# Granule 4's values one piece sooner and its last norm ahead of the key copies, mask tables later, two PSUM banks changed in granule 2, and three squares moved to VectorE

## The chip, the cores and the metric

One core of a Trainium2 chip. The metric is device time in microseconds (us) of one execution; lower is better. A run lists the time and the span from the first to the last instruction; the time is about 1.8 us more than the span.

## The reference, cut to what matters

```python
scores = q @ k.T / sqrt(64) - slope[h] * dist          # 4 batches, 8 heads, 768 positions
scores = where(is_global | is_local, scores, -1e9)     # 8 global keys, 96 local ones
a = exp(scores - max); a = a / (sum(a) + 1e-9)
x = (a @ v)  as 3072 x 512
h = maximum(x @ w_in, 0)                               # 512 x 2048
out = (s * h * h + b) @ w_out                          # 2048 x 512
```

## The kernel before: the parts concerned

The kernel works through 12 granules of 256 positions. Granule j+1's attention is interleaved by hand with the first product (P1, eight pieces) of granule j and the second product (P2) of granule j-1. The order of the calls is the order of the instructions on every engine. Terms: `SS` makes scores (PE), exponentials (ACT) and masked weights (DVE); `A` multiplies by the values and then normalises (DVE); `KO`/`VO` copy neighbouring keys and values (DVE); `XT_dma`/`XT_pe` transpose the normalised result for P1; `T_ev` copies transposes out of PSUM; `make_tmpl(h)` makes one head's mask table (ACT); `Q` squares a P1 piece later on (DVE); `W_tw` subtracts blocks of output weights for the later granules (DVE, below "table difference"); `P2_bias` adds the bias to an output (DVE). PE is TensorE, ACT ScalarE, DVE VectorE.

```python
ps_h  = tc.tile_pool(name="ps_h",  bufs=2, space=PSUM)   # "psh": two buffers
ps_o  = tc.tile_pool(name="ps_o",  bufs=1, space=PSUM)   # "pso": one
ps_av = tc.tile_pool(name="ps_av", bufs=1, space=PSUM)   # "av": one
...
def P1(j, fp, sq="dve", tag="psh"):
    ...                                  # 8 matmuls into ps
    flush()                              # squares that wait in `pend` (DVE)
    nc.scalar.activation(gs, ps, Relu)   # ACT
    if sq == "act":    nc.scalar.activation(gs, gs, Square)
    elif sq == "late": late_sq[j, fp] = gs     # Q(j, fp) squares it on DVE later
    else:              pend.append(gs)
...
    def period(j, items, at, late=None, mid=()):     # j = 3 and 4
        SS(j, (0, 1));  run(items, at[0])
        A(j, 0);        run(items, at[1])
        A(j, 1, "psh"); run(list(mid), 100)
        SS(j, (2, 3));  run(items, at[2])
        A(j, 2)
        KO(j + 1)
        run(items, at[3])
        A(j, 3, "psh")
        if late is None: XT_dma(j)
        ...                                          # VO, XB, then the rest of items
```

Later granules (`steady`) run a tighter loop, which the change leaves alone; its first P1 piece of granule 4 reads what `XT_dma(4)` made.

The softmax here doesn't subtract the row's maximum and nothing guards it: scores larger than these inputs give would overflow.

## Time and profile before

| | before |
|---|---|
| time, three runs at first | 210.44 us median (210.06 to 210.52) |
| span of the profiled run | 207.9 us |
| PE busy | 200.8 us (97%) |

To read it: a P1 matmul's row is 0.273 us long on average, but the next one starts 0.109 us after it, so rows overlap and "busy" hides short stops. PE's losses below are therefore from start to start, as in the prediction (usual spacing 0.109 us for 256 columns, 0.216 for 512). A gap of one spacing exactly inside a group of four or eight is a missing record, not a stop: this trace has all 2291 matmuls.

### The profile page before, as it was taken

The numbers are of one execution on the slowest core, as the hardware profiler recorded it, in microseconds if no ns is written. First come the engines' busy times: TensorE is split into PE (matmuls) and PEld (weight loads), VectorE is DVE, ScalarE is ACT, GpSimd is POOL, SyncE is SP. The second block draws the span as 40 slices with busy tenths as digits, with TensorE's granted clock in tenths as the row PEclk, the third lists the DMA queues.
The fourth block names the chain that finished last, engine by engine and source line by source line (L and its number), as shares of the span: only waits on it lengthen the run. The fifth ranks groups of instructions, "written<-read, shape, count | busy, mean of one in ns | idle before, by whom it ended". The sixth has DMA issues, their size and how long they took to land.

```text
span 207.9 us, 5598 instructions
## 1 busy us (share of the span) xinstructions
PE 200.8 (97%) x2291; PEld 160.8 (77%) x2291; DVE 167.9 (81%) x404; ACT 119.8 (58%) x184; POOL 75.5 (36%) x98
## 2 busy tenths in 40 slices
PE   7999999999999998999999999999999999999992
PEld 2667866557666777888988988988978988988882
DVE  3776567599889998788799799788799799787683
ACT  5779899345978784636536536546356456425300
POOL 8985673937364006509029019037000000000000
PEclk9999999999999999999999999999999999999999
DMA  5999999999999976999969959959946040040022
GB/s 165 193 184 198 188 196 190 182 145 160 134 131 166 182 133 85 183 144 132 209 93 118 208 83 119 207 101 120 193 79 176 3 151 4 0 151 3 2 104 101
DMA packets 103850, 27.64 MB, mean 133 GB/s; under 512 B 91408, under 2 KB 101904, under 8 KB 103824
## 3 DMA queue, kind: packets, MB, share of 16 engines
q0 software_dynamic: 70976, 13.11, 86.3%
q1 hardware_dynamic: 31792, 13.64, 32.1%
q10 hardware_dynamic: 1056, 0.52, 0.9%
q8 instruction: 18, 0.29, 0.6%
q14 instruction: 8, 0.07, 0.1%
HBM read 27.26 MB, written 6.29 MB: 161 GB/s over the span
## 4 chain that ended last, share of the span: by engine, by line
PE 79%; ACT 9%; DVE 5%; DMA 4%; issue 2%; SPq 0%; ACTq 0%; DVEq 0%
PE ps L528 35%; PE ps_w L690 14%; PE ps_wb L690 6%; PE ps L589 6%; PE ps_av L446 4%; PE ps_s L395 4%; PE ps_wa L690 3%; ACT pt L408 3%; ACT gT L538 2%; DMA xT<-xn 2%; DMA raw<-in_k_dram 2%; PE ps_s L379 2%; PE ps_2s L589 2%; DVE xn L464 1%; ACT gT L546 1%
## 5 line engine op out<-in xcount | busy, mean ns | idle before, releaser
L528 PE MATMUL ps<-xT,w_in_bf 128*128 128x256 bf16 x768 | 96.5, 273 | 1.0 <-DMA xT<-xn 0.6
L528 PEld LDWEIGHTS <-w_in_bf 128*128 128x128 bf16 x768 | 72.9, 98 | 12.4 <-DMA xT<-xn 0.9
L540 ACT ACTIVATE gT<-ps 128x512 bf16<-128x512 f32 x72 | 43.0, 598 | 59.1 <-PE ps L528 56.3
L408 ACT ACTIVATE pt<-ps_s 128x1024 bf16<-128x1024 f32 (+1 forms) x48 | 43.0, 952 | 2.0 <-PE ps_s L395 2.0
L690 PEld LDWEIGHTS <-sw 128*128 128x128 bf16 x288 | 28.1, 98 | 3.4
L418 DVE TENSOR_TENSOR pt<-pt,tmpl 128x1024 bf16<-128x1024 bf16 (+1 forms) x40 | 25.2, 647 | 2.9 <-ACT pt L408 2.4
L556 DVE TENSOR_TENSOR gT<-gT 128x512 bf16<-128x512 bf16 x66 | 25.1, 416 | 1.8 <-ACT gT L540 1.6
L690 PEld LDWEIGHTS <-gT 128*128 128x128 bf16 x216 | 20.5, 98 | 3.3 <-issue 0.2
L112 POOL DMA_DIRECT2D vaug<-in_v_dram x24 | 21.5, 911 | 4.1 <-DMA w_out_bf<-in_moe_w_out_dram 1.7
L125 POOL COPY pdum<-xT 1x1 bf16<-1x1 bf16 x5 | 4.7, 944 | 48.6 <-DMA xT<-xn 48.6
L464 DVE TENSOR_TENSOR xn<-ps_av,rc 128x256 bf16<-128x256 f32 x48 | 20.4, 425 | 1.7
L589 PE MATMUL ps<-w_out_bf,gT 128*128 128x512 bf16 x80 | 19.7, 379 | 0.0
L690 PE MATMUL ps_w<-tw,sw 128*128 128x256 bf16 x144 | 18.7, 272 | 0.0
L700 DVE SCALAR_TENSOR_TENSOR u<-ps_w,s_bc,bvec 128x256 f32<-128x256 f32 x27 | 12.9, 480 | 6.7 <-PE ps_w L690 6.7
L446 PEld LDWEIGHTS <-pt 128*128 128x128 bf16 x352 | 15.3, 98 | 3.3 <-DVE xn L464 1.0
L104 POOL DMA_DIRECT2D qnat<-in_q_dram x18 | 16.1, 905 | 2.8 <-DMA w_out_bf<-in_moe_w_out_dram 1.4
L538 ACT ACTIVATE gT<-ps 128x512 bf16<-128x512 f32 x24 | 14.2, 598 | 4.4 <-PE ps L528 4.4
L446 PE MATMUL ps_av<-vaug,pt 128*128 128x65 bf16 x224 | 16.4, 193 | 0.3 <-DVE xn L464 0.2
L104 POOL DMA_DIRECT2D knat<-in_k_dram x18 | 16.0, 894 | 1.2 <-issue 1.0
L463 DVE RECIPROCAL rc<-ps_av 128x4 f32<-128x4 f32 x48 | 8.7, 182 | 9.2 <-PE ps_av L446 9.0
L589 PEld LDWEIGHTS <-gT 128*128 128x128 bf16 x96 | 8.6, 98 | 8.2
L395 PE MATMUL ps_s<-qT,kT 64*128 64x128 bf16 x224 | 12.4, 218 | 0.0
(94 smaller groups left out, 241.1 us busy)
## 6 DMA issues: line engine op xcount, KB each, us to landing
out_dram<-o_pr SPq DMA_DIRECT2D x8, 512.0 KB, 4.1
vaug<-in_v_dram POOLq DMA_DIRECT2D x24, 128.0 KB, 7.8
knat<-in_k_dram POOLq DMA_DIRECT2D x22, 128.0 KB, 5.7
qnat<-in_q_dram POOLq DMA_DIRECT2D x22, 128.0 KB, 7.7
w_in_bf<-in_moe_w_in_dram POOLq DMA_DIRECT2D x8, 256.0 KB, 8.2
w_out_bf<-in_moe_w_out_dram POOLq DMA_DIRECT2D x4, 512.0 KB, 9.9
out_dram<-o_pr SPq DMA_DIRECT2D x7, 256.0 KB, 5.3
raw<-in_q_dram ACTq DMA_DIRECT2D x2, 256.0 KB, 4.9
```

What stands on the lines that cost most here:

```text
L104: nc.gpsimd.dma_start(t[:, i, :, :], src[b, :, sb * P : (sb + 1) * P, :].rearrange("h p d -> p h d"))
L112: nc.gpsimd.dma_start(vaug[b % 2][:, sb, :, 0:D], v[b, :, sb * P : (sb + 1) * P, :].rearrange("h p d -> p h d"),)
L395: nc.tensor.matmul(ps[:, hi, oc * P : (oc + 1) * P], lhsT=kt[r, :], rhs=qT[j][r, hp, i * P : (i + 1) * P], start=not biased, stop=not bias ...
L408: nc.scalar.activation(pt[:, :, 0:n], ps[:, :, 0:n], ACT.Exp, scale=QSCALE)
L418: nc.vector.tensor_tensor(pt[:, :, 0:n], pt[:, :, 0:n], m, ALU.mult)
L446: nc.tensor.matmul(av[:, i, hi, :], lhsT=pt[:, hi, c * P : (c + 1) * P], rhs=vv, start=n_ == 0, stop=n_ == len(ops) - 1,)
L464: nc.vector.tensor_tensor(xn[j][:, :, 2 * hp : 2 * hp + 2, :], av[:, :, :, 0:D], rc[:].to_broadcast((P, GB, 2, D)), ALU.mult,)
L528: nc.tensor.matmul(ps[:, i, :], lhsT=w_in_bf[:, kc, fc * P : (fc + 1) * P], rhs=xT[j][:, kc, :], start=(kc == 0), stop=(kc == KC - 1),)
L540: nc.scalar.activation(gs.rearrange("p f (r t) -> p f r t", r=2), ps[:].rearrange("p f (t r) -> p f r t", r=2), ACT.Relu,)
L556: nc.vector.tensor_tensor(gs, gs, gs, ALU.mult)
L589: nc.tensor.matmul(po[j, tb], lhsT=gT[j][:, fc, tb * P : (tb + 1) * P], rhs=w_out_bf[:, fc, :], start=(fc == 0), stop=(fc == FC - 1),)
L690: nc.tensor.matmul(wt[j, ps], lhsT=lhs[:, f, :], rhs=rhs[:, f, :], start=first and f == 0, stop=f == HF - 1, skip_group_check=True,)
```

## The change

Its intent: ACT makes mask tables when PE does not wait for it; granule 2's last values need not wait for a norm in the same bank; granule 4's normalised result is ready sooner, so that its DMA transposes land before P1 asks for them. One square of granule 3's period and two of granule 4's go from ACT to DVE.

```diff
+    P1(1, 2)
+    P1(1, 3)
     make_tmpl(2)
-    P1(1, 2)
-    make_tmpl(3)
-    P1(1, 3)
     P1(0, 6)
-    make_tmpl(4)
     T_quads(2, "k", ("pso", "av"))
...
     T_ev(2, 1, "q", "act")
+    make_tmpl(3)
     P1(1, 4)
     KO(2)
     VO(2)
-    make_tmpl(5)
+    make_tmpl(4)
     P1(1, 5)
     SS(2, (0, 1))
     P1(1, 6)
     P1(1, 7)
+    make_tmpl(5)
     make_tmpl(6)
...
-    A(2, 3)
+    A(2, 3, "psh")
...
-    XT_pe(2, "act", "psh")
+    XT_pe(2, "act", "av")
...
         A(j, 2)
-        KO(j + 1)
+        if at[3]:
+            KO(j + 1)
         run(items, at[3])
         A(j, 3, "psh")
+        if not at[3]:
+            KO(j + 1)
...
-            (P1, 2, 4, "act"),
+            (P1, 2, 4),
...
-   items += [(P2, l, 5), (P2_bias, 1, 0), (P1, m, 2, "act"), (P2, l, 6), (P1, m, 3, "act"), (P1, m, 4, "act")]
-   items += [(P2, l, 7), (P1, m, 5, "act"), ...]
-   period(j, items, (4, 3, 3, 0), mid=...)
+   items += [(P2, l, 5), (P2_bias, 1, 0)]
+   items += [(P1, m, 2, "late"), (P1, m, 3, "late"), (P2, l, 6), (Q, m, 2), (Q, m, 3)]
+   items += [(P1, m, 4, "act"), (P2, l, 7), (P1, m, 5, "act"), ...]
+   period(j, items, (4, 2, 3, 0), mid=...)
```

More of the change, by code (lines that the diff above doesn't have):

```diff
@@ L1074 @@
             items = [(P1, m, 0, "act"), (P2, l, 4), (P1, m, 1), (W_tw, 2, 0, 4)]
-            items += [(P2, l, 5), (P2_bias, 1, 0), (P1, m, 2, "act"), (P2, l, 6), (P1, m, 3, "act"), (P1, m, 4, "act")]
-            items += [(P2, l, 7), (P1, m, 5, "act"), (P1, m, 6), (W_tw, 4, 0, 4), (P1, m, 7), (W_sw, m, 3), (flush,), (W_tw, 4, 4, 8)]
-            period(j, items, (4, 3, 3, 0), mid=((W_tw, 2, 4, 8), (P2_bias, 1, 1, False)))
+            items += [(P2, l, 5), (P2_bias, 1, 0)]
+            items += [(P1, m, 2, "late"), (P1, m, 3, "late"), (P2, l, 6), (Q, m, 2), (Q, m, 3)]
+            items += [(P1, m, 4, "act"), (P2, l, 7), (P1, m, 5, "act"), (P1, m, 6), (W_tw, 4, 0, 4), (P1, m, 7), (W_sw, m, 3), (flush,), (W_tw, 4, 4, 8)]
+            period(j, items, (4, 2, 3, 0), mid=((W_tw, 2, 4, 8), (P2_bias, 1, 1, False)))
         else:
```

## The prediction

> **What bounds the kernel now.** I read the page's first part, then the chain that ended last, then the table of windows, then the timeline of the tensor engine (PE) beside those of VectorE (DVE) and ScalarE (ACT). The busy shares first:
>
> ```profile
> PE 200.8 (97%) x2291; PEld 160.8 (77%) x2291; DVE 167.9 (81%) x404; ACT 119.8 (58%) x184; POOL 75.5 (36%) x98
> ```
>
> PE is busy for 97%, and the chain of waits is PE for 79%. No matmul is added or removed by the change, so it can win only time in which PE stands still. The windows (us: length, then busy time of PE, PEld, DVE, ACT, POOL) show where that could be:
>
> ```profile
> 20.00:30.00 10.00, 9.66 (x152) 8.13 (x151) 5.82 (x15) 9.12 (x17) 7.36 (x10) 1.00 1.57 193
> ...
> 60.00:70.00 10.00, 10.00 (x110) 6.43 (x109) 9.69 (x21) 6.81 (x11) 4.66 (x6) 1.00 2.32 143
> 70.00:80.00 10.00, 9.18 (x98) 7.02 (x96) 9.36 (x21) 8.18 (x12) 0.19 (x1) 1.00 0.95 160
> 80.00:100.00 20.00, 19.94 (x241) 17.61 (x239) 16.42 (x42) 11.15 (x18) 11.68 (x14) 1.00 1.38 143
> ```
>
> From 20 to 30 us ACT is the full engine (9.12 of 10); from 60 to 80 us it is DVE (9.69 and 9.36); after 80 us PE hardly stops. So the change, which touches only granules 2, 3 and 4, has 20 to 80 us to work on. Four lines of PE's timeline there carry its waits (in brackets: idle time, releaser):
>
> ```profile
> 29.00 0.44 PE L288 MATMUL ps_t<-ident,qnat 64*64 64x64 bf16 x30 [0.28 <-ACT kT L308]
> ...
> 40.48 0.20 PE L446 MATMUL ps_av<-vaug,pt 128*128 128x65 bf16 x1 [0.18 <-DVE xn L464]
> ...
> 56.72 1.91 PE L528 MATMUL ps<-xT,w_in_bf 128*128 128x256 bf16 x16 [0.15 <-ACT gT L538]
> ...
> 79.74 1.92 PE L528 MATMUL ps<-xT,w_in_bf 128*128 128x256 bf16 x16 [0.61 <-DMA xT<-xn]
> ```
>
> The brackets understate the loss, as a matmul is still shown busy while its result drains. I therefore took it from start to start: in the chain of waits eight L528 matmuls take 0.87 us, so 0.109 apart; four L589 take 0.86. The distance to the next start, less the matmul's own spacing, gives the loss: 0.49 at 28.50-29.00 (q transposes of granule 2), 0.21 at 26.18 (a P1 piece), 0.35 at 40.48 (last values of granule 2), 0.36 at 56.72, 0.31 at 72.59 (last values of granule 4), 0.77 at 79.74 (first P1 of granule 4, which needs the transposed xn). About 2.5 us in all; that is the ceiling of what the change aims at.
>
> Granule 4 stands under a second bound, which decides the size:
>
> ```profile
> 69.30 0.42 DVE L464 TENSOR_TENSOR xn<-ps_av,rc 128x256 bf16<-128x256 f32 x1
> ...
> 69.64 0.68 DVE L651 TENSOR_TENSOR tw<-w_out_bf,tw 128x1024 bf16<-128x1024 bf16 x1
> ...
> 70.24 0.69 DVE L627 TENSOR_TENSOR o_pr<-o_pr,bvec 128x512 f32<-128x512 f32 x1
> ...
> 70.93 0.69 DVE L418 TENSOR_TENSOR pt<-pt,tmpl 128x1024 bf16<-128x1024 bf16 x1
> ...
> 71.85 0.69 DVE L418 TENSOR_TENSOR pt<-pt,tmpl 128x1024 bf16<-128x1024 bf16 x1 [0.22 <-ACT pt L408]
> ```
>
> The reader is to see that each begins where the last ends: DVE itself, not its inputs, sets when the masked weights for the last values are ready; only 0.22 of it is a wait for ACT.
>
> **What the Trainium skill says.** "Perfetto Trace Analysis", Identifying the Most-Contended Engine, says matmul busy share is no good measure, and under Optimization Strategy that regimes with different full engines are to be found and the gaps read one by one; the windows agree, with three regimes. "PSUM — Partial Sum Buffer", PSUM bank collisions raise a hardware error, says two engines may not touch one bank and quadrant at once, even at different columns. That fits the 29.00 line: the q transposes write another half of the tile that ACT still copies k from, and they wait for that copy. "Perfetto Trace Analysis", Matmuls, wants independent groups in different banks so that eviction overlaps the next group; the 40.48 line is that case missed, two value pieces in the single "av" buffer. "ScalarE: Activation LUTs", Rules for kernel authors, prefers DVE for multiplication: the trace agrees (square 0.63 us on ACT, about 0.42 on DVE), but it helps only where DVE has room.
>
> **The change, part by part.**
>
> *Mask tables later (20 to 38 us).* Eight tables stay eight. An exp for a table occupies ACT for 0.62 us start to start, an eviction 0.49 to 0.60. Now three tables stand before granule 2's k copy on ACT, afterwards one. By hand: the evictions of P1(1,2) and P1(1,3) go at 25.29 and 26.17 instead of 25.54 and 26.64; the P1 piece at 26.18 starts at 25.97; one table from 26.66 to 27.28, one eviction to 27.77, then the k copy until 28.35 (28.95 before). The q transposes can finish from about 28.4 instead of 29.00, so the next P1 piece goes at 28.75 instead of 29.37: 0.62 won. But the two tables moved ahead of granule 2's exponentials, and DVE's work, take a part back: its first score exponential goes at about 31.6 instead of 32.05, 0.46 won. Three squares on DVE (34.63 to 35.72 before) and one norm then let the second values start at 35.9 instead of 36.37. The tables that now wait behind, 5 to 7, end at about 36.4 and the next scores arrive at 36.75, so this third table on ACT is free. Left of this part: about 0.45 us.
>
> *Granule 2's last values in another bank.* At 40.48 they waited for the norm of the pair before in the same bank. "psh" has two buffers, one held by an output sum, the other free. 0.35 us is won. The transposes in "av" find that bank free, as its reader is through; they cost nothing. Sum up to 48 us: **0.8 us**.
>
> *Granule 3, one square to DVE.* ACT loses 0.63 us at 55.56, but the next eviction waits on its own matmuls until about 55.98 and went at 56.09: **0.1 us** won. DVE takes the 0.42 us in a hole of 0.41 before the norm at 56.17.
>
> *Granule 4.* Before the last values there is one P1 piece fewer (0.87 us), and the norms pass the key copies (0.42 and 0.18). Two squares leave ACT (2 x 0.63) and come to DVE (2 x about 0.4). I follow DVE, on the clock of the kernel before: the norm at 69.09 already came straight after DVE's bias from 68.49, so earlier values don't speed it. It runs on through table sum and bias to the masked weights, which come at 71.65 and 72.25 instead of 71.62 and 72.54; the first is unchanged; at the second the 0.22 wait for ACT goes, with the instruction start-up that it exposed: 0.3 won. PE, now at the values by 71.2, waits about 0.5 there and 0.4 at the last ones, more than the 0.31 before. Then the last norm, no longer behind the key copies, ends at 73.35 instead of 74.22, so the xn transposes start about 0.9 us sooner and, if they take as long, land near 78.8 instead of 79.69. PE has 0.87 us more work to do until it needs them, arrives at 72.25 + 6.15 + 0.87 = 79.3 (6.15: from 72.59 to 78.97, where the wait for the transposes began, less 0.23 at 78.1 for a square), and does not wait: 79.74 - 79.3, about **0.45 us** won of the 0.77. Its squares after the values put DVE a little later, but the piece they feed starts at 78.4 and needs the last square at 78.1.
>
> Sum: 0.8 + 0.1 + 0.45 = 1.35 us. I take 0.15 off for the first rival: **1.2 us**, 210.44 - 1.2 = **209.2 us**.
>
> **The rivals.** *A transfer becomes the wait.* Granule 3's q transposes land by the trace's landing events at 48.87 and 50.67 us, PE needs them at 51.68; 0.8 us sooner is 50.9, so 0.2 us of slack remain, and loads of granule 5, paced by an output piece, start sooner and share the DMA engines. Each transpose takes about 2 us there. One late half microsecond would leave only about 0.9 us of gain in all: 209.5. *DVE becomes the bound outright in granule 4.* It gets 3 squares more between 55 and 76 us. If they delay granule 5's masking, which stands behind them, the gain there goes to nothing: 209.6 to 210. For it: 9.69 busy of 10; against it: 80 to 100 us has DVE at 16.42 of 20, and the values of granule 5 need the masking only at 81. *PE absorbs all.* The steady stage is PE-bound, so what comes before should carry to the end unchanged; but if its loads or the two-buffer "psh" re-form the same bubble, the result is 210.4. *The full ceiling:* all of 26-80 us vanishing would give about 208.
>
> **Range and chances.** Runs before lie within 210.06 to 210.52, so 0.25 us is noise. Full working plus a bit of luck gives 208.6, the two rivals together 210.2. Range 208.5 to 210.3. Faster by over 2% would need 4.2 us, more than the 2.5 that stand still; slower by as much would need a wait that no order here shows. So within 2%: 0.98.
>
> **What would show it.** In the changed profile: the k copy on ACT done near 28.4 and the wait of the q transposes nearly gone; the last values of granule 2 unreleased by a norm; xn's transposes issued near 72.5 us (74.29 less 0.9 for the earlier norm and 0.9 won before this stage) and no DMA wait of PE at the first P1 of granule 4; in its place waits of the values for DVE's masked weights. After 80 us the same steps, shifted. The prediction is wrong if PE waits for granule 3's transposes near 51 us, if DVE's chain from 62 to 72 us shrinks more than I think, or if the steady stage opens gaps.

## The result, and the profile after

The changed kernel took **208.20 us** (median of 4 runs, 208.09 to 208.29), beside 210.25 us for the kernel before (4 runs, 209.66 to 210.52). The ratio is 0.9906 (95% interval 0.9882 to 0.993). Ratios here are the mean time of one kernel's fast runs over that of the other's in the same rounds, so not quite the ratio of the medians. It is the same by the 2% mark, faster by 0.9%, and below the forecast range (208.5 to 210.3).

The busy shares after, and the same windows as before (length, then busy PE, PEld, DVE, ACT, POOL):

```profile
PE 199.6 (97%) x2283; PEld 160.6 (78%) x2291; DVE 168.7 (82%) x407; ACT 118.4 (57%) x181; POOL 73.9 (36%) x98
```

```profile
20.00:30.00 10.00, 10.00 (x155) 8.51 (x151) 6.30 (x16) 8.43 (x17) 7.31 (x10) 1.00 1.56 193
...
60.00:70.00 10.00, 9.71 (x105) 6.52 (x106) 9.73 (x21) 7.16 (x11) 3.70 (x5) 1.00 2.04 147
70.00:80.00 10.00, 9.75 (x102) 7.49 (x102) 9.40 (x22) 6.33 (x10) 3.52 (x5) 1.00 1.19 172
80.00:100.00 20.00, 19.94 (x240) 17.60 (x238) 16.56 (x43) 11.21 (x18) 7.67 (x10) 1.00 1.47 144
```

What to see: PE's loss left the stretches 20 to 30 us and shrank from 70 to 80 us (9.18 busy before, 9.75 after), a smaller one came up at 60 to 70 us, where PE had been full, and DVE is still full there. PE's timeline after, at the places of the four lines quoted in the prediction and at two new ones:

```profile
28.20 0.55 PE L288 MATMUL ps_t<-ident,qnat 64*64 64x64 bf16 x32
...
39.59 0.19 PE L446 MATMUL ps_av<-vaug,pt 128*128 128x65 bf16 x1
...
55.75 0.49 PE L528 MATMUL ps<-xT,w_in_bf 128*128 128x256 bf16 x3
...
68.81 1.05 PE L528 MATMUL ps<-xT,w_in_bf 128*128 128x256 bf16 x8 [0.18 <-DVE xn L464]
...
71.21 0.20 PE L446 MATMUL ps_av<-vaug,pt 128*128 128x65 bf16 x1 [0.18 <-DVE pt L418]
...
78.46 0.71 PE L528 MATMUL ps<-xT,w_in_bf 128*128 128x256 bf16 x5
```

The q transposes are one unbroken group now (0.11 us lost from start to start, 0.49 before); the last values of granule 2 follow the matmuls ahead of them at once; the first P1 of granule 4 (last line) names no DMA. In return a P1 piece waits at 68.81 for a norm on DVE, which holds its PSUM buffer (0.34 us start to start), and the last values of granule 4 wait for masked weights at 71.21 (0.34 us, 0.31 before).

ACT in the kernel before, then after, up to granule 2's k copy (L308):

```profile
26.02 0.74 ACT L255 ACTIVATE tmpl<-base 128x640 bf16<-128x640 bf16 x1
26.64 1.21 ACT L538 ACTIVATE gT<-ps 128x512 bf16<-128x512 f32 x2
27.75 0.73 ACT L255 ACTIVATE tmpl<-base 128x640 bf16<-128x640 bf16 x1
28.37 0.58 ACT L308 COPY kT<-ps_t 128x512 bf16<-128x512 bf16 x1
```

```profile
26.58 0.73 ACT L255 ACTIVATE tmpl<-base 128x640 bf16<-128x640 bf16 x1
27.20 0.59 ACT L538 ACTIVATE gT<-ps 128x512 bf16<-128x512 f32 x1
27.68 0.59 ACT L308 COPY kT<-ps_t 128x512 bf16<-128x512 bf16 x1
```

The copy ends 0.68 us sooner by the clock (28.95 against 28.27); 0.09 of it was there at the unchanged P1 piece at 21.6 us. DVE in the kernel before at granule 4's key copy and last norm, and the issue of its xn transposes (SPq is SyncE, which issues DMAs):

```profile
73.05 0.42 DVE L339 COPY ko<-kT 128x1024 bf16<-128x1024 bf16 x1
...
73.80 0.42 DVE L464 TENSOR_TENSOR xn<-ps_av,rc 128x256 bf16<-128x256 f32 x1
...
74.29 2.51 SPq L507 DMA_TRANSPOSE xT<-xn  x2
```

And after, with the last masks:

```profile
69.87 1.28 DVE L418 TENSOR_TENSOR pt<-pt,tmpl 128x1024 bf16<-128x1024 bf16 x2
...
71.89 0.42 DVE L464 TENSOR_TENSOR xn<-ps_av,rc 128x256 bf16<-128x256 f32 x1
72.23 0.42 DVE L339 COPY ko<-kT 128x1024 bf16<-128x1024 bf16 x1
...
72.38 2.50 SPq L507 DMA_TRANSPOSE xT<-xn  x2
```

The key copy now follows the last norm, and the transposes are issued 1.9 us sooner by the clock. By the trace's landing events the second one landed at 76.11 us, 79.69 before. From marks of PE (starts of matmuls that both kernels have in the same order), the length of each stage:

| stage, between starts on PE | before | after | won |
|---|---|---|---|
| P1(0,5), at 21.6 us, to P1(0,6) | 4.58 | 4.38 | 0.20 |
| to granule 2's first scores | 5.04 | 4.66 | 0.38 |
| to its second scores | 5.48 | 5.62 | -0.14 |
| to its xn transposes | 4.89 | 4.53 | 0.36 |
| to granule 3's scores | 10.08 | 10.08 | 0 |
| to granule 4's scores | 11.58 | 11.52 | 0.06 |
| to granule 5's scores | 13.17 | 13.63 | -0.46 |
| to the first P1 of granule 4, 79.7 us before | 3.31 | 2.54 | 0.77 |
| to the same place in the next period, 94 us | 14.42 | 14.41 | 0.01 |

Together 1.2 us (94.16 - 21.60 less 92.87 - 21.51). Of the -0.46, the two waits of 0.34 us less the 0.31 of before make 0.37, and another 0.06 lies at the values between them. The 1.2 us are less than the 2.05 us between the medians. Whence the rest, and whether each part does what the table says, was for the experiments.

### The profile page after: what moved, and what is told of

It is laid out like the page before. It is cut to its first block, busy times and chain, and to the rows that moved or that the text cites. A ratio compares the mean times of both kernels' runs of the same rounds, so it can differ in the third digit from the quotient of the medians.

```text
span 206.5 us, 5590 instructions
## 1 busy us (share of the span) xinstructions
PE 199.6 (97%) x2283; PEld 160.6 (78%) x2291; DVE 168.7 (82%) x407; ACT 118.4 (57%) x181; POOL 73.9 (36%) x98
## 4 chain that ended last, share of the span: by engine, by line
PE 83%; DVE 8%; DMA 3%; ACT 3%; issue 1%; POOL 0%; SPq 0%; DVEq 0%; ACTq 0%; POOLq 0%
PE ps L528 37%; PE ps_w L690 14%; PE ps_wb L690 6%; PE ps L589 6%; PE ps_s L395 5%; PE ps_av L446 5%; PE ps_wa L690 4%; DMA raw<-in_k_dram 2%; PE ps_s L379 2%; DVE xn L464 2%; PE ps_2s L589 2%; DVE pt L418 2%; ACT pt L408 1%; DMA xT<-xn 1%; DVE o_pr L627 1%
## 5 line engine op out<-in xcount | busy, mean ns | idle before, releaser
L556 DVE TENSOR_TENSOR gT<-gT 128x512 bf16<-128x512 bf16 x68 | 25.8, 415 | 1.8 <-ACT gT L540 1.6
L112 POOL DMA_DIRECT2D vaug<-in_v_dram x24 | 21.6, 918 | 4.4 <-DMA w_out_bf<-in_moe_w_out_dram 1.7
L125 POOL COPY pdum<-xT 1x1 bf16<-1x1 bf16 x5 | 3.2, 648 | 49.2 <-DMA xT<-xn 49.2
L589 PE MATMUL ps<-w_out_bf,gT 128*128 128x512 bf16 x74 | 18.8, 379 | 0.4 <-issue 0.2
L395 PE MATMUL ps_s<-qT,kT 64*128 64x128 bf16 x224 | 12.5, 218 | 0.0
```

The lines of the kernel that those rows point to most:

```text
L112: nc.gpsimd.dma_start(vaug[b % 2][:, sb, :, 0:D], v[b, :, sb * P : (sb + 1) * P, :].rearrange("h p d -> p h d"),)
L395: nc.tensor.matmul(ps[:, hi, oc * P : (oc + 1) * P], lhsT=kt[r, :], rhs=qT[j][r, hp, i * P : (i + 1) * P], start=not biased, stop=not bias ...
L556: nc.vector.tensor_tensor(gs, gs, gs, ALU.mult)
L589: nc.tensor.matmul(po[j, tb], lhsT=gT[j][:, fc, tb * P : (tb + 1) * P], rhs=w_out_bf[:, fc, :], start=(fc == 0), stop=(fc == FC - 1),)
```

## The experiments

All ran correct. Sixteen runs of eleven kernels (the kernel before and the changed one among them); the first twelve runs in three sets of five rounds beside the kernel before, the last four as looks. The sets ran on chips 12, 14 and 10, the looks on chip 11. Each run left one trace, so the stages of one kernel rest on one trace; for the kernel before there are six traces, for the changed one three.

### Is the gain as large as first measured?

**The kernel before against itself** (no edit):

> The kernel before, unchanged, against itself. Theory A (the forecast's sum was right in size and the four runs of before were scattered: 209.66 to 210.52): same, ratio within 0.2% of 1, and times around 209.7. Theory B (before is really about 210.3 and its profiled run, 209.63, was a lucky one): same ratio, but times of 210.2 to 210.5, and a trace with a span near 208.5 instead of 207.9, which should then show an extra wait of 0.5 to 0.8 us, most likely for the xn transposes of granule 4 or granule 3's q transposes.

Ratio 1.0009 (0.9988 to 1.003); 210.01 us (209.49 to 210.29), beside 209.89 (209.32 to 210.38) in the same rounds. Its trace repeats the table's stages within 0.01 us up to 80 us; then it loses 0.45 us at one P1 piece at 94 us, waiting for xn transposes. The times lie between the two theories.

**The changed kernel again** (no edit), in two sets:

> The changed kernel again, with more rounds. Theory A: 1.1 to 1.4 us below before in the same rounds (ratio 0.9935 to 0.9948), the sum of the shifts that the two traces show in granules 2 to 4. Theory B: 2.0 us below (ratio 0.9906).

Ratio 0.9932 (0.991 to 0.9954), 208.48 us: 1.4 us below before. As theory A said; its stages again sum to 1.2 us.

> The changed kernel again, to settle the size of the gain: the traces' steps add to 1.2 us, while its ten runs so far lie 1.5 us below before by the span. If the steps are all there is, the ratio here is near 0.994 (1.2 to 1.3 us); if before loses more to late DMA landings in the runs that were not profiled, it stays near 0.9925 (1.5 us or more).

Ratio 0.9922 (0.9892 to 0.9951), 208.56 us. The third set doesn't settle it by itself: before had one run of 211.59 in it, and before's mean was 210.18 us, against 209.83 and 209.78 in the other two sets. Its stages, from 21.6 to 94 us, last 71.33 us, against 72.56 before: 1.23 us.

### The parts of granule 2

**Tables and banks** (both edits of granule 2, nothing else):

> Only the tables moved and granule 2's last values and transposes in other PSUM banks. Theory A: 0.65 us below before (the two traces: 0.90 us of shift at 41 us, of which 0.26 was there before the first changed instruction). Forecast: 0.8 us. Theory B, if the missing 0.8 us sits in this part: 1.4 us or more.

Ratio 0.9981 (0.9947 to 1.0015), with one run of 211.05 among six. Its trace gives the stages of the changed kernel: 0.81 us won between 21.6 and 51.6 us. But in this very run PE had stood still for 0.95 us just before, at 22.3 us, at a piece that no edit touches and that needs the sixth part of w_in; that part landed at 22.30 instead of 21.49. So one stop in a load hid most of the gain in the span (207.5 us against 207.9).

**Tables alone** (only the moved `make_tmpl` and P1 calls):

> The kernel before with only the mask tables moved. Forecast: 0.45 us below before. In the trace from the first changed piece to the transposes of granule 2's xn: 0.20 at the P1 piece, 0.38 at the q transposes, 0.14 given back before the second scores, so 0.44 kept. Rival (the gain is eaten at granule 2's last values, which wait for a norm in the same bank): less than 0.2.

Stages: 0.20, 0.38, -0.14, then 0: 0.44 us. The last values still wait 0.35 us for the norm in their bank. Ratio 0.9951 (0.9921 to 0.998).

**Banks alone**:

```diff
-    A(2, 3)
+    A(2, 3, "psh")
-    XT_pe(2, "act", "psh")
+    XT_pe(2, "act", "av")
```

> The kernel before with only granule 2's last values and transposes in other PSUM banks. Forecast: 0.35 us below before; in the trace exactly the step at granule 2's last values, nothing elsewhere. Rival: the values then wait for their masked weights instead: under 0.2.

Stages: 0.36 us at that place and nothing elsewhere. Ratio 0.9956 (0.9923 to 0.9988). Both parts' stages are as forecast and add up (0.44 + 0.36 = 0.80). Both ratios say more (about 1.0 and 0.9 us), but they share the rounds in which before was slow: without its run of 211.59 they would be 0.9 and 0.8 us, and against its mean in the other two sets about 0.6.

### The parts of granule 4

**Both parts** (the new piece order, norms first):

> Only granule 4: values one piece sooner, norms ahead of the key copies, two squares to VectorE. Theory A: 0.3 to 0.5 us below before (shift 0.97 at 62 us to 1.29 at 80 us). Theory B, if before usually loses more at the xn transposes than in its profiled run: 1.0 us or more.

Ratio 0.9981 (0.9959 to 1.0003). Stages: -0.46, then 0.77 won: 0.31 us.

**Norms first alone** (`KO` behind `A(j, 3, "psh")`, old piece order):

> The kernel before with one change: in granule 4 the last norm goes ahead of the key copies. Reading of the traces: the last norm ends 0.55 us sooner, so do the xn transposes, and PE's 0.77 us wait at the first P1 piece of granule 4 shrinks by as much: 0.5 us below before, more than all of granule 4's changes together (0.3). Rival: the copies are not what holds the transposes (the DMA engines are, which took 4.15 us for the second one): under 0.2 us.

```profile
79.45 0.72 PE L528 MATMUL ps<-xT,w_in_bf 128*128 128x256 bf16 x5 [0.40 <-DMA xT<-xn]
```

The line is PE's first P1 of granule 4. PE still waits for the DMA, 0.56 us start to start. The last transpose was issued at 74.93 instead of 75.54, but took 4.48 us instead of 4.15, so the stage won 0.2 us, not 0.5. This expectation failed: what the norm gives sooner, the transfer partly takes back. By 94 us even the 0.2 was gone: PE lost 0.21 us there, where the next granule's xn transposes landed at 93.95 us. Ratio 0.9977 (0.995 to 1.0005).

**Values sooner alone** (the new piece order, `KO` before the last norm):

> The kernel before with only the piece order of granule 4 changed (one P1 piece moved behind the values, two squares to VectorE), the key copies still ahead of the last norm. Reading of the traces: 0.3 us below before, as much as with the norms first, because one more piece behind the values covers the transposes anyway, while PE now waits 0.35 us for a norm in a PSUM buffer that it did not need before. Rival (both parts are needed): PE still waits for the transposes and under 0.1 us is won.

Stages: -0.46 and 0.77, the whole 0.31 us. The trace held the expectation with a hair's breadth: the second transpose landed at 79.70 and PE asked for it at 79.91. The ratio, 0.9999 (0.9979 to 1.0019), shows nothing, and in this trace PE again stood still before 22 us (0.76 us at w_in). With the norms first the landing is at 76.11 and PE's need at 78.46: so the order gives the gain and both together the margin. The trace of both parts without granule 2's edits says how (landing 77.32, need 79.69): about 0.5 us of the margin is the earlier issue, 1.65 us a shorter transfer (2.47 us against 4.12), whose cause is open.

**All but the new piece order**:

> The changed kernel with granule 4's old piece order: tables, banks, one square and norms first. Reading of the traces: 0.8 + 0.1 + 0.5 = 1.4 us below before, so 0.2 us below the changed kernel. Rival: parts overlap and it is slower than the changed kernel.

PE's wait for the transposes fell to 0.27 us, so granule 4 won 0.5 us in this trace and the stages from 21.5 to 79 us sum to 1.4, against 1.2 for the changed kernel. By time it isn't faster, as far as sets can be compared (the changed kernel ran in the other two): 208.49 us, ratio 0.9941 (0.9921 to 0.9961). It still depends on a landing of 4.2 us. A trace alone would have picked the wrong one, or none: the two differ by less than runs do.

### Is DVE full, or only in the wrong order?

**DVE relieved**: in the changed kernel, what stands in DVE's queue ahead of the norm and the masks of granule 4 goes behind the values.

```diff
-   items += [(P2, l, 5), (P2_bias, 1, 0)]
-   items += [..., (P2, l, 6), (Q, m, 2), (Q, m, 3)]
-   items += [(P1, m, 4, "act"), (P2, l, 7), ..., (W_sw, m, 3), (flush,), (W_tw, 4, 4, 8)]
-   period(j, items, (4, 2, 3, 0), mid=((W_tw, 2, 4, 8), (P2_bias, 1, 1, False)))
+   items += [(P2, l, 5)]
+   items += [..., (P2, l, 6), (P2_bias, 1, 0), (Q, m, 2), (Q, m, 3)]
+   items += [(P1, m, 4, "act"), (P2, l, 7), (P2_bias, 1, 1, False), ..., (flush,), (W_sw, m, 3)]
+   period(j, items, (4, 1, 3, 0))
    # in steady(5): W_tw(2, 4, 8) before A(5, 1), W_tw(4, 4, 8) before the masks of its last values
```

> The changed kernel, with the work that stands in VectorE's queue ahead of granule 4's norm and masks moved behind the values (two bias adds, one table difference; the other difference into granule 5), and the last square ahead of a difference. If VectorE's order, and not its total work, holds PE there, the waits of 0.35 us (P1 piece for a PSUM buffer), 0.34 us (last values) and 0.23 us (product for the last square) go: up to 0.9 us below the changed kernel, ratio to before near 0.989. Rival: VectorE is full, and granule 5 pays the same time back: no faster than the changed kernel.

Granule 4's scores to the first P1 took 15.40 us instead of 16.17: 0.77 won, and the two 0.34 us waits are gone (that for the square, 0.23, stayed). But granule 5 gave 0.65 back:

```profile
85.66 0.20 PE L446 MATMUL ps_av<-vaug,pt 128*128 128x65 bf16 x1 [0.18 <-DVE pt L418]
```

Its last values wait 0.55 us in two steps for masked weights that stand behind the moved table difference. 208.34 us, ratio 0.9936 (0.9913 to 0.9958): no better than the changed kernel in its own sets (0.9932 and 0.9922). The rival was right for this placing.

**DVE relieved, second placing** (that difference behind granule 5's norms instead):

```diff
-        if j == 5: W_tw(4, 4, 8)
         S_mul(j, 2)
...
         W_post(l, 7)
+        if j == 5: W_tw(4, 4, 8)
         r(5)
```

> The relieved kernel, with the table difference that stood ahead of granule 5's last masks moved behind its norms. The trace of the relieved kernel showed the 0.55 us that it gave back at those masks. If they are the only place, it is 0.5 us below the relieved kernel and about 0.7 us below the changed one (ratio to before near 0.990). Rival: VectorE is full and the wait turns up elsewhere in granule 5 or 6.

**208.03 us** (207.57 to 208.46), ratio 0.9897 (0.9867 to 0.9928): the best of all, about 0.5 us below the changed kernel in the same rounds (means 208.06 and 208.56). The waits for masks are gone from granule 5; in its trace PE waits once more for a landing:

```profile
92.93 0.82 PE L528 MATMUL ps<-xT,w_in_bf 128*128 128x256 bf16 x6 [0.21 <-DMA xT<-xn]
```

The stages from 21.6 to 94 us now last 70.92 us, against 71.33 in the changed kernel's trace of the same set: 0.77 us won in granule 4, 0.37 lost again to that landing. So in this trace DVE was in the wrong order rather than out of time. The 0.5 us by time lies within the overlap of the two intervals; 0.4 us of it the stages place.

### Where do the kernel before's runs scatter?

Four looks at the kernel before, unchanged:

> The kernel before, one profiled look, to catch a slow one of its runs (spans of 207.5 to 209.8 us so far). Theory J (jitter of DMA landings that the change does not touch): a long run is long before 22 us (first loads, w_in) or at 94 and 155 us (xn transposes), and its stages between 22 and 80 us last as in the first trace, within 0.05. Theory K (the changed stages themselves scatter): a long run loses it at granule 2's transposes or granule 4's xn transposes, where the wait of 0.77 then grows to 1.0 or more.

> As the first look: J, excess before 22 us or at 94 and 155 us; K, excess between 22 and 80 us.

> As the first look: J, excess before 22 us or at 94 and 155 us; K, excess between 22 and 80 us.

> As the first look: J, excess before 22 us or at 94 and 155 us; K, excess between 22 and 80 us.

They took 209.20, 209.43, 210.19 and 209.28 us. From 21.6 to 94 us all four last 72.57 to 72.59 us (72.56 in the first trace): nothing that the change touches scatters, and the wait for granule 4's transposes is always 0.77 to 0.79. The slow look lost its time at the untouched piece before 22 us:

```profile
22.07 5.19 PE L528 MATMUL ps<-xT,w_in_bf 128*128 128x256 bf16 x44 [0.61 <-DMA w_in_bf<-in_moe_w_in_dram]
```

Its stage up to there, from a P1 piece at 12.5 us, took 9.54 us instead of 8.76 in the first trace. At 155 us it lost 0.14 us (0.24 in the first trace), so that place doesn't set it apart. Theory K fell; theory J held for the one long run that was caught. The longest run, 211.59, has no trace.

## Why the prediction was right or wrong

- **The bound.** Right where the change acts: between 20 and 80 us PE's stops were for ACT first, then for DVE, and at 79.74 for a DMA landing. From 80 us on the first trace has three stops of 0.24 to 0.28 us. No kernel's stages won more than 1.65 of the 2.5 us named as the ceiling.
- **Tables later, "about 0.45 us".** Right, and by its own steps: 0.58 us won up to the first scores, 0.14 given back, 0.44 kept; tables alone show it. The k copy ended at 28.36 on the clock of the kernel before (28.27 and the 0.09 us that the run was ahead at 21.6), 28.35 by hand.
- **Another bank, "0.35 us".** Right: 0.36, alone and together. The reason drawn from the Trainium skill's "Perfetto Trace Analysis", Matmuls, agrees with the trace: the group that rotates to another bank no longer names the norm.
- **Granule 3, "0.1 us".** Right in kind: 0.06 to 0.09.
- **Granule 4, "about 0.45 us".** Mechanism right, size too large: 0.31. The transposes did leave the path (0.77 won there) and DVE's waits did take a part of it. Of the terms, the waits "about 0.5 there and 0.4 at the last ones" measured 0.34 at the P1 piece, which I had only inside the first of them, and 0.34; the wait for the last square, which I let vanish, stayed at 0.23. That is the term that was mis-sized. PE arrived at 79.43 on the clock of the kernel before, not at 79.3: 0.23 more for the square, 0.07 less for last values that started sooner than forecast. The transposes landed 2.35 us ahead of need, not half a microsecond, since the second took 2.5 us and not 4.15.
- **The 0.15 us taken off for the first rival.** Wrong: no wait of note came at granule 3's scores (0.07 us in one trace, where the q transposes landed at 50.81 us; none in the other two). "Each transpose takes about 2 us there" misreads the trace: the two were issued 2.06 us apart, but took 7.24 and 6.99 us from issue to landing. DVE as outright bound didn't come either.
- **The sum, 1.35 us, forecast as 1.2.** The stages measure 1.2 us, in three traces of the changed kernel. That 1.2 itself was met is partly luck: 0.14 too much for granule 4 and 0.15 taken off for a rival that didn't come cancel.
- **The time, 209.2, and the range down to 208.5: wrong.** The step that failed is the base and its scatter, on which sum and range stand: "Runs before lie within 210.06 to 210.52, so 0.25 us is noise." Three runs gave neither the level nor the scatter. The kernel before has since run between 209.20 and 211.59 us, with medians of 209.83 to 209.90 in the three sets; 210.44 lies some 0.55 us above them. That mis-sized base is about 0.55 of the 1.0 us between 209.2 and 208.20. Another 0.3 is that the first four runs of the changed kernel were low: its later sets have medians of 208.48 and 208.56. About 0.15 us is left beside 209.85 - 1.2 = 208.65. The chief source of scatter that a trace caught, the w_in landing, lies ahead of every changed instruction.
- **What stays open.** By time the changed kernel lies 1.3 to 2 us below before in three sets, and its intervals reach from 1.0 to 2.5 us; the stages up to 94 us give 1.2. After that the changed kernel's three traces are longer by 0.23 us in the mean (113.80 and 113.56 us), with losses of 0.18 to 0.43 us at a P1 piece near 154 us that follows xn transposes (0 to 0.24 before). By the profiled runs alone the gain is 1.0 us (means 209.62 of six and 208.61 of three), by the runs without a profile 1.6 (209.96 of 43 and 208.37 of 13). So beside the 1.2 us, 0.2 to 0.4 us of the mean gain in the two later sets, and 0.8 in the first, is placed in no stage. The changed kernel's fastest run and before's fastest, 208.09 and 209.20, differ by 1.1 us, which speaks for chance in the slow runs; that it is chance is argued, not shown, as only profiled runs have a trace.

## What to carry to other kernels

Forecast a small change stage by stage between marks that both traces share; from 21.6 to 80 us such stages repeated here to some hundredths of a microsecond in six traces, while whole runs of the same kernel lay up to 2.4 us apart. Take the scatter from an A/A comparison before naming a range: a few runs that agree say little about the next ones. When a wait on a transfer is removed by moving work, look at what the moved work queues behind on the next-fullest engine, and test an order before calling that engine full.

## What the Trainium skill lacked or had wrong

- "Perfetto Trace Analysis", Identifying the Most-Contended Engine, warns of matmul busy share, but has no recipe for the stops that it hides. From start to start, the wait at 79.74 is 0.77 us; the idle time in brackets was 0.61, and at 40.48 it was 0.18 for 0.35.
- No page that I read tells how much the time to landing of the same DMA transpose depends on what is around it: the second of granule 4's two took 4.15 to 4.19 us in six traces of the kernel before, 2.46 to 2.49 in three of the changed one, and 4.48 with the norms first alone, at the same size. Why is open.
- No page that I read tells an engine that is full from one whose queue is in the wrong order. Here DVE was busy for 9.73 of 10 us from 60 to 70 us, and yet moving work off the front of its queue won 0.77 us in granule 4's stages.
